# The residual of a channel MLP: turned to token layout by VectorE block transposes and SBUF moves in place of TensorE transposes

## The chip, the cores and the metric

The kernel runs on one core of one Trainium2 chip. The metric is the device time of one execution in microseconds (us). Unless marked ns, every time below is in us. All tensors that the engines compute with are 32-bit floats.

The engines are named as in the profile: PE is TensorE (PEld its weight loads), DVE is VectorE, ACT is ScalarE, POOL is GpSimd, SP is SyncE, which only issues transfers (DMAs). "SPq" and "ACTq" are the queues in which SP and ACT issue them.

## What is computed

```python
# 8 batch rows, 8 heads, 576 tokens, head size 64
scores = matmul(q, k.T) / 8
thresh = max(scores, -1) - tau
scores = where(scores >= thresh, scores, -1e9)
attn   = softmax(scores)                    # exp(scores - max) / (sum + 1e-9)
x      = matmul(attn, v)                    # heads side by side: (8, 576, 512)
# token MLP, over the 576 tokens of a row
u      = x + (relu(x.T @ w_tok1) @ w_tok2).T     # 576 -> 256 -> 576
# channel MLP, over the 512 channels of a token
out    = u + relu(u @ w_ch1) @ w_ch2             # 512 -> 1536 -> 512
```

What matters here is the last line: `u`, the residual, is needed twice. As input of the first channel product it is needed with the channels on the partitions; as addend of the output it is needed with the tokens on the partitions.

## The kernel before, in words

**Attention.** The work goes in 144 units (line 84): a batch row, a pair of head pairs, and one of 9 query tiles. Per unit, `scores` (L289) multiplies q and k for two heads into PSUM (L303), VectorE takes the row maxima (L308) and GpSimd makes the bias of them (L309). `weigh` (L312) has ScalarE apply the threshold (L318) and the exponential (L325); `norm` (L329) divides. The weights must then be turned. In row 0 TensorE does it (`turn`, L341). From row 1 on `turn_blocks` (L358) does it: VectorE transposes 32x32 blocks in place of their order (L366), and when three units are together 16 transfers on SP's queue (L375), one for each pair of block row and block column, carry the blocks to where they belong, from `T` to `eT`. `values` (L392) multiplies the turned weights with v (L410, L415) two units later; x comes out with channels on the partitions, in `xTs`, one tile for two batch rows.

**Token MLP.** `token_mlp` (L427) turns x on TensorE (L446), does the two products (L453, L463) and adds the result to x (L467). So `uT`, the residual, lies in `xTs` with channels on the partitions: 4 chunks of 128 channels, 1152 tokens of two rows.

**Channel MLP.** `channel_mlp` (L476) works on groups of 256 tokens (`GR`); two rows have 1152 tokens, so each pair of rows has four groups of 256 and one of 128. A group has 12 steps `ch1(j)` (L487, 128 of the 1536 hidden channels each, ReLU on ScalarE in L488) and, for each tile of 128 tokens, four steps `ch2(t, part)` with three of the 12 hidden chunks each (L503), which add up in one PSUM tile with the tokens on the partitions. Here is how the residual enters: in part 0, before the products, TensorE transposes the four 128x128 chunks of `uT` into this PSUM tile (L499, `start=(c == 0), stop=False`), and the products are added on top. After part 3, VectorE copies the tile to `o` (L508), and SP stores it (L509). There are 36 tiles of 128 tokens, thus 144 transposes. `o` has two buffers.

**Order.** The order of all instructions is written by hand. The MLP's steps stand in a queue `todo`, each with a cost (0.0067 us per token for a `ch1`, 2.6 or 3.0 us for a `ch2`). `fill` (L524) takes steps from it between the pieces of the attention's unit, to a quota per unit that `push` (L537) computes from the sum of the costs. So while the attention of row b runs, TensorE also does the MLPs of the rows before. What is left when the attention ends is done in one stretch (L655). Engines run their own instructions strictly in order, SP's queue too. q and k loads are issued by ScalarE from row 1 on (L644), v loads by SP (L646).

**Weights.** The MLP weights arrive as 64-bit floats and are converted in 31 pieces during rows 0 and 1, in steps on ScalarE (L192, L194), VectorE (L202, L204, L208) and GpSimd (L216). The raw words lie in a tile `scratch`, which has room for four pieces and 512 words more. One intermediate, `h2`, is written by L194 and read by L202 and L204; it is taken from the buffers of `o` (L180).

Of the kernel before, what the change touches and what calls it, by code (L numbers as in the profile page):

```python
# [9 lines left out]
F32 = mybir.dt.float32  # L10
# [7 lines left out]
P = 128  # L18
# [3 lines left out]
def kernel(  # L22
# [25 lines left out]
    nc = tc.nc  # L48
    B, H, S, D = q.shape
    DM = H * D  # L50
# [10 lines left out]
    NCC = DM // P  # L61
    NJ = DCH // P
    HS = S // 2
    NK = 2 * S // P
    GR = 2 * P
# [4 lines left out]
    work = ctx.enter_context(tc.tile_pool(name="work", bufs=2))  # L70
# [39 lines left out]
    def load_v(n):  # L110

        b, p = pairs[n]
        lv = ld.tile([P, NK, D], F32, tag="lv", bufs=4, name=f"lv_{n}")
        nc.sync.dma_start(out=lv, in_=v[b].rearrange("h s d -> (h s) d")[2 * S * p : 2 * S * p + 2 * S, :].rearrange("(c p) d -> p c d", p=P))
        vals[n] = lv
# [11 lines left out]
    wc2 = const.tile([P, NJ, DM], F32, name="wc2")  # L127
# [8 lines left out]
    WMAX = 512  # L136
    scratch = work.tile([P, NP * 2 * S], U32, tag="xT", name="scratch")
    NRAW = 4
    raw_at = [scratch[:, 2 * WMAX * i : 2 * WMAX * (i + 1)] for i in range(NRAW)]

    def like(x, dst):
        if len(dst.shape) == 2:
            return x
        return x.rearrange("p (a b) -> p a b", a=dst.shape[1])
# [23 lines left out]
    def load_piece(i):  # L168
        if i >= len(pieces):
            return  # L170
        dst, src = pieces[i]
        rows = dst.shape[0]
        n = 1
        for d in dst.shape[1:]:
            n *= d
        raw = raw_at[i % NRAW][0:rows, 0 : n * (2 if wide(i) else 1)].bitcast(src.dtype)
        nc.sync.dma_start(out=like(raw, dst), in_=src)
        if wide(i):
            words = raw.bitcast(U32).rearrange("p (n w) -> p n w", w=2)
            h2 = work.tile([P, WMAX], F32, tag="o", name=f"h2_{i}")[0:rows, 0:n]  # L180
            raws[i] = like(words[:, :, 0], dst), like(words[:, :, 1], dst), like(h2, dst)
        else:
            raws[i] = like(raw, dst)

    def wide(i):
        return i < len(pieces) and pieces[i][1].dtype == I64
# [37 lines left out]
    def weight(n):  # L224

        nonlocal steps_done
        for k in range(steps_done, min(steps_done + n, 3 * len(pieces) + 1)):
            i, part = divmod(k, 3)
            if part == 0:
                on_gpsimd(i - 1)  # L230
                if i:
                    load_piece(i - 1 + NRAW)
            else:
                on_scalar(i + 1, part - 1)
            on_vector(i, part)
            steps_done = k + 1

    def weight_to(x):

        weight(max(int(x) - steps_done, 0))  # L240

    def need(i):

        weight(3 * i + 4 - steps_done)

    load_piece(0)
    load_v(0)
    for i in range(1, NRAW):
        load_piece(i)
# [27 lines left out]
    def in_blocks(b):  # L277
        return b > 0
# [60 lines left out]
    GU = 3  # L339
# [87 lines left out]
    def token_mlp(b, ps=range(NP)):  # L427
# [45 lines left out]
        steps += [(0.97, lambda c=c, f=f: tok2(c, f)) for c in ps for f in range(2)]  # L473
        return steps, (first, first + NTK)

    def channel_mlp(b, uT, i):  # L476

        s = {}
        n = min(GR, 2 * S - GR * i)

        def ch1(j):
            need(7 + j)
            if j == 0:
                s["g"] = work.tile([P, NJ, GR], F32, tag="g", bufs=1, name=f"g_{b}_{i}")
            ps = ps_mm.tile([P, GR], F32, tag="mm", name=f"c1_{b}_{i}_{j}")[:, 0:n]
            for c in range(NCC):
                nc.tensor.matmul(ps, lhsT=wc1[:, j, c, :], rhs=uT[:, c, GR * i : GR * i + n], start=(c == 0), stop=(c == NCC - 1))  # L487
            nc.scalar.activation(out=s["g"][:, j, 0:n], in_=ps, func=AF.Relu)  # L488

        def ch2(t, part):  # L490
            need(7 + NJ + 3 * part + 2)
            t0 = GR * i + P * t
            if part == 0:
                s["ps"] = ps_mm.tile([P, NCC, P], F32, tag="mm", name=f"c2_{b}_{i}_{t}")
            ps = s["ps"]
            flat = ps.rearrange("q c d -> q (c d)")
            if part == 0:
                for c in range(NCC):
                    nc.tensor.matmul(  # L499
                        ps[:, c, :], lhsT=uT[:, c, t0 : t0 + P], rhs=ident, is_transpose=True, start=(c == 0), stop=False, skip_group_check=True  # L500
                    )
            for j in range(3 * part, 3 * part + 3):
                nc.tensor.matmul(  # L503
                    flat, lhsT=s["g"][:, j, P * t : P * t + P], rhs=wc2[:, j, :], start=False, stop=(j == NJ - 1), skip_group_check=True
                )
            if part == 3:
                o = work.tile([P, DM], F32, tag="o", name=f"o_{b}_{i}_{t}")
                nc.vector.tensor_copy(out=o, in_=flat)  # L508
                nc.sync.dma_start(out=out[b : b + 2].rearrange("b s d -> (b s) d")[t0 : t0 + P, :], in_=o)  # L509

        return [(0.0067 * n, lambda j=j: ch1(j)) for j in range(NJ)] + [
            (2.6 if part else 3.0, lambda t=t, part=part: ch2(t, part)) for t in range(n // P) for part in range(4)
        ]

# [43 lines left out]
    def values_due(u):  # L560
        while due and due[0][0] <= u:
            _, b, p0, g = due.popleft()
            values(b, p0, g)
            if b == 0 and p0 == 0 and g == 2:
                return True
            if p0 == NP - 2 and g == 2:
                if not in_blocks(b):
                    return True
                push(b)
        return False  # L570

    for u in range(len(units) + LAG + 4):
        on = u < len(units)
        if u == UB:
            late.close()
            ps_mm = ctx.enter_context(tc.tile_pool(name="ps_mm", bufs=2, space=bass.MemoryType.PSUM))
        if on:
            b_now, p0, t = units[u]
            n = b_now * NP + p0
        w = u - LAG  # L580
        back = 0 <= w < len(units)
        if on:
            scores(u)

        last = False
        visit = False
        if due and not in_blocks(due[0][1]):
            visit = due[0][0] <= u
            last = values_due(u)
        elif early:  # L590
            early.popleft()[1]()
        if 0 < u <= len(units):
            norm(u - 1)
        if b_now:
            weight(2)
        else:


            weight_to(2.25 * (u - (1 if visit else 1.5)))
            if visit and on:  # L600
                weigh(u)
        while copies:
            copies.popleft()()
        if last and u < UB:
            early.extend(token_mlp(0, range(NP // 2))[0])
        elif last:
            push(0)
        if back:
            wb, wp, wt = units[w]
            if not in_blocks(wb):  # L610
                for i in range(3):
                    turn(w, i)
            if wt % GU == GU - 1:
                g = wt // GU
                if g < 2:
                    split_middle(wb * NP + wp + g)
                due.append((u + (2 if in_blocks(wb) else 1), wb, wp, g))
        if b_now:
            fill(0.4)
        if back and in_blocks(wb):  # L620
            turn_blocks(w)
        if b_now:
            weight(2)
        if on and (b_now or not visit):
            weigh(u)
        elif b_now:
            fill(0.6)
        if b_now:
            weight(2)
        elif u == 0:  # L630
            on_scalar(0, 0)
            on_scalar(0, 1)
        else:
            weight_to(2.25 * (u - 1))
        if on:


            when = {3: (2, 0, 2), 4: (2, 2, 4), 5: (2, 4, 6), 6: (2, 6, 8), 8: (3, 0, 3), 0: (1, 3, 6), 1: (1, 6, 8)}
            if u == 0:
                load_qk(1, (nc.sync, nc.sync), range(0, 3))  # L640
            if t in when:
                m, lo, hi = when[t]
                if n + m < len(pairs):
                    load_qk(n + m, (nc.scalar if b_now else nc.sync,) * 2, range(lo, hi))  # L644
            if t in (3, 7) and n + 2 + t // 4 < len(pairs):
                load_v(n + 2 + t // 4)  # L646
            if t == 2:
                prep(n + 1)
            if t == 7 and n + 2 < len(pairs):
                prep(n + 2)  # L650
        if due and in_blocks(due[0][1]):
            values_due(u)
    need(len(pieces) - 1)
    quota = 1e9
    fill(1.0)  # L655
# [28 lines left out]
```

## Time and profile before

| | before |
|---|---|
| median of 3 runs (lowest to highest) | 1362.69 (1360.92 to 1366.38) |
| the profiled execution: its own time | 1362.23 |
| the profiled execution: span of the profile | 1360.1 |
| mean clock granted to TensorE | 0.996 |
| DVE, ACT, POOL busy, share of the span | 42%, 43%, 26% |
| the four heaviest lines of PE: L503, L487 (256 columns), L303 (128 columns), L415 (384 columns) | 390.6, 350.0, 172.5, 89.1 |
| the transposes of the residual, L499, x144: sum of their durations | 22.0 |
| copies to `o`, L508, x36: busy, mean | 24.7, 687 ns |
| attention's block transposes, L366, x126: busy, mean | 172.1, 1366 ns |

The span is the time from the first to the last record of one profiled execution; the execution's own time has some 2.1 us around it. A busy sum of TensorE counts the durations of overlapping instructions once per instruction in the groups, but the engine's total counts every instant once. A matmul's duration is not what it costs the engine, since the next one begins before it has ended; the distance from start to start is. In timelines a line gives the start in us, the length in us, then engine, line, operation and names; square brackets at the end give the idle time before it and who ended it. In views of waits a line reads: who waited, for whom, total us, number of times, longest.

### The profile page before, as it was taken

Reading aid. Unit: us, or ns where it says so; the run is one execution under the profiler, and the core shown is the slowest. Engines: PE = TensorE matmul, PEld = TensorE weight load, DVE = VectorE, ACT = ScalarE, POOL = GpSimd, SP = SyncE. Lnnn points to the kernel's source line nnn. Section 1 sums busy time; section 2 is a strip of 40 time slices with the busy share of each in tenths; the row PEclk is TensorE's granted clock in tenths of the full one; section 3 lists DMA queues with packets and bytes.
Section 4 is the critical chain, followed back from the end, with each engine's and each line's share of the span. In section 5 each row is a group of like instructions: output and inputs, shape, how many; then the busy total and the mean of one; then the engine's idle time right before and its main releaser. Section 6 shows DMA issues by size and latency. Waiting matters only on the chain.

```text
span 1360.1 us, 17717 instructions
## 1 busy us (share of the span) xinstructions
PE 1315.2 (97%) x6246; PEld 817.2 (60%) x6246; DVE 575.3 (42%) x1009; ACT 584.3 (43%) x1299; POOL 353.6 (26%) x683
## 2 busy tenths in 40 slices
PE   6888899999999999999999999999999999999998
PEld 4555556547474666655665566565756566576675
DVE  5878874445443434443333454434333443201000
ACT  6776664445454444543434445353434444120010
POOL 4666653222222222221212222222212222100000
PEclk9999999999999999999999999999999999999999
DMA  5434774545453533533244444435333442400000
GB/s 122 109 92 129 196 170 102 127 95 127 96 130 77 134 89 84 135 76 92 66 112 99 104 97 114 95 76 118 90 90 74 114 99 70 111 0 16 8 16 16
DMA packets 278871, 128.20 MB, mean 94 GB/s; under 512 B 200896, under 2 KB 271552, under 8 KB 278784
## 3 DMA queue, kind: packets, MB, share of 16 engines
q1 hardware_dynamic: 150176, 111.06, 32.0%
q10 hardware_dynamic: 128608, 16.01, 7.4%
q8 instruction: 50, 0.82, 0.3%
q14 instruction: 37, 0.30, 0.1%
HBM read 43.25 MB, written 9.44 MB: 39 GB/s over the span
## 4 chain that ended last, share of the span: by engine, by line
PE 89%; DVE 4%; DMA 2%; ACT 2%; issue 1%; SPq 1%; POOL 1%; ACTq 0%; DVEq 0%; POOLq 0%
PE c L503 28%; PE c L487 27%; PE sc L303 11%; PE pv L415 8%; PE t L453 5%; PE t L463 4%; PE pv L410 3%; DVE mx L308 2%; PE c L499 1%; PE tx L446 1%; PE tr L354 1%; ACT e L318 1%; SPq L375 1%; DMA eT<-T 1%; DMA lk<-in_k_dram 1%
## 5 line engine op out<-in xcount | busy, mean ns | idle before, releaser
L308 DVE TENSOR_REDUCE mx<-sc 128x1 f32<-128x576 f32 x288 | 204.5, 750 | 484.6 <-PE sc L303 484.6
L487 PE MATMUL c<-xT,wc 128*128 128x256 f32 (+1 forms) x1920 | 400.3, 362 | 0.1
L503 PE MATMUL c<-wc,g 128*128 128x512 f32 x864 | 390.6, 597 | 0.0
L487 PEld LDWEIGHTS c<-xT,wc 128*128 128x128 f32 x1920 | 334.4, 191 | 70.5 <-issue 31.5
L309 POOL TENSOR_SCALAR bias<-mx,toff 128x1 f32<-128x1 f32 x288 | 81.9, 284 | 781.2 <-DVE mx L308 724.3
L318 ACT ACTIVATE e<-sc,bias 128x576 f32<-128x576 f32 x288 | 199.4, 740 | 157.5 <-POOL bias L309 153.5
L503 PEld LDWEIGHTS c<-wc,g 128*128 128x128 f32 x864 | 157.4, 190 | 175.4 <-issue 173.7
L488 ACT ACTIVATE g<-c 128x256 f32<-128x256 f32 (+1 forms) x240 | 86.8, 362 | 321.4 <-PE c L487 308.6
L325 ACT ACTIVATE e<-e,ntau 128x576 f32<-128x576 f32 x288 | 221.1, 772 | 0.0
L336 POOL TENSOR_SCALAR e<-e,rr 128x576 f32<-128x576 f32 x288 | 214.6, 757 | 14.7 <-DVE rr L333 2.8
L303 PE MATMUL sc<-kT,qT 64*128 64x288 f32 (+1 forms) x1280 | 193.5, 441 | 11.9 <-DVE kT L285 7.2
L366 DVE STREAM_TRANSPOSE T<-e 128x1152 f32<-128x1152 f32 x126 | 172.1, 1366 | 5.8 <-DMA eT<-T 3.6
L303 PEld LDWEIGHTS sc<-kT,qT 64*128 64x128 f32 (+1 forms) x1280 | 106.2, 181 | 99.2 <-issue 61.8
L415 PE MATMUL pv<-eT,lv 128*64 128x384 f32 (+1 forms) x1024 | 136.2, 406 | 0.0
L415 PEld LDWEIGHTS pv<-eT,lv 128*64 128x64 f32 x1024 | 75.2, 137 | 49.3 <-issue 40.4
L508 DVE COPY o<-c 128x512 f32<-128x512 f32 x36 | 24.7, 687 | 169.7 <-PE c L503 169.7
L420 ACT COPY xT<-pv 128x384 f32<-128x384 f32 (+1 forms) x56 | 21.0, 400 | 166.2 <-PE pv L415 165.2
L463 PE MATMUL t<-w,a 128*128 128x288 f32 x256 | 73.6, 414 | 5.7 <-DVE xT L467 4.8
L453 PE MATMUL t<-x_sb,w 128*128 128x512 f32 (+1 forms) x180 | 73.4, 555 | 0.0
L467 DVE TENSOR_TENSOR xT<-xT,t 128x288 f32<-128x288 f32 x64 | 28.4, 448 | 86.6 <-PE t L463 86.0
L463 PEld LDWEIGHTS t<-w,a 128*128 128x128 f32 x256 | 45.5, 190 | 28.0 <-issue 11.7
L325 ACT ACTIVATION_READ_ACCUMULATOR e<-e,ntau 128x1 f32 x288 | 56.8, 197 | 0.0
(44 smaller groups left out, 547.2 us busy)
## 6 DMA issues: line engine op xcount, KB each, us to landing
eT<-T SPq DMA_DIRECT2D x672, 108.0 KB, 2.3
scratch<-in_moe_w_ch_dram SPq DMA_DIRECT2D x24, 512.0 KB, 3.8
lv<-in_v_dram SPq DMA_DIRECT2D x32, 288.0 KB, 3.5
out_dram<-o SPq DMA_DIRECT2D x36, 256.0 KB, 2.2
lk<-in_k_dram ACTq DMA_DIRECT2D x111, 72.0 KB, 2.7
lq<-in_q_dram ACTq DMA_DIRECT2D x106, 72.0 KB, 2.3
lq<-in_q_dram SPq DMA_DIRECT2D x22, 72.0 KB, 3.2
lk<-in_k_dram SPq DMA_DIRECT2D x17, 72.0 KB, 3.4
```

What stands on the lines that cost most here:

```text
L303: nc.tensor.matmul(sc[h][rows, f, 0:HS], lhsT=qT[r, cols], rhs=kT[r, HS * f : HS * f + HS], start=True, stop=True)
L308: nc.vector.tensor_reduce(out=mx[:, c], in_=sc[h][:, :, 0:HS], axis=AX.XY, op=ALU.max)
L318: nc.scalar.activation(out=eh, in_=sc[h][:, :, 0:HS], func=AF.Prelu, bias=bias[:, h : h + 1], scale=SCALE, alpha=STEEP)
L325: nc.scalar.activation(out=eh, in_=eh, func=AF.Exp, bias=ntau, accum_out=rs[:, h : h + 1])
L336: nc.gpsimd.tensor_scalar(out=eh, in0=eh, scalar1=rr[:, h : h + 1], scalar2=1.0, op0=ALU.mult, op1=ALU.mult)
L366: nc.vector.transpose(out=T[:, :, place, :].rearrange("p a (c x) -> p c a x", c=NK), in_=e.rearrange("p (c a x) -> p c a x", c=NK, a=4))
L415: nc.tensor.matmul(to[r], lhsT=lv[:, j, :], rhs=e[j], start=False, stop=(c == NI - 1), skip_group_check=True)
L453: nc.tensor.matmul(to, lhsT=w1[:, t, P * m : P * m + P], rhs=x_sb[:, t, cols], start=(t == 0), stop=(t == NT - 1))
L463: nc.tensor.matmul(to, lhsT=a[:, m, P * c : P * c + P], rhs=w2[:, m, HS * f : HS * f + HS], start=(m == 0), stop=(m == NTK - 1))
L487: nc.tensor.matmul(ps, lhsT=wc1[:, j, c, :], rhs=uT[:, c, GR * i : GR * i + n], start=(c == 0), stop=(c == NCC - 1))
L488: nc.scalar.activation(out=s["g"][:, j, 0:n], in_=ps, func=AF.Relu)
L503: nc.tensor.matmul(flat, lhsT=s["g"][:, j, P * t : P * t + P], rhs=wc2[:, j, :], start=False, stop=(j == NJ - 1), skip_group_check=True)
```

## The change

From the third batch row on (`b` is 2, 4 or 6 in `channel_mlp`, which counts pairs of rows), the four transposes on TensorE are left out, and the first product begins the PSUM tile. In their place, `turn_u` transposes the 32x32 blocks of the group's `uT` on VectorE into a tile `us`, at the step `ch1(1)`. It puts 16 moves in a list; each carries a block row and a block column from `us` to `ut`. The list is emptied to SP's queue by `move_u`: at the end of the first of each three attention units, at the end of every unit once no new scores are begun, and before the first eviction that needs them. At the eviction VectorE adds PSUM and `ut` in one instruction and writes to `us`, whose own content has been moved by then; the store reads it there. `us` and `ut` have one buffer each, for a whole group of up to two tiles. Rows 0 and 1 keep the transposes and the copy, but their copy goes to `us` as well.

The buffers of `o` are gone. `h2` therefore moves to the 512 spare words of `scratch`, of which there is one in place of two.

```diff
+    high = scratch[:, 2 * WMAX * NRAW : 2 * WMAX * NRAW + WMAX].bitcast(F32)
...
-            h2 = work.tile([P, WMAX], F32, tag="o", name=f"h2_{i}")[0:rows, 0:n]
+            h2 = high[0:rows, 0:n]
...
+    moves = deque()
+
     def channel_mlp(b, uT, i):
 
         s = {}
         n = min(GR, 2 * S - GR * i)
+        nt = n // P
+
+        def turn_u():
+
+            us, ut = s["us"], s["ut"]
+            nc.vector.transpose(
+                out=us[:, 0:nt].rearrange("q n a (c d) -> q c (n a) d", c=NCC),
+                in_=uT[:, :, GR * i : GR * i + n].rearrange("q c (m r) -> q c m r", r=32),
+            )
+
+            def move(a, k):
+                nc.sync.dma_start(out=ut[32 * a : 32 * a + 32, 0:nt, k, :], in_=us[32 * k : 32 * k + 32, 0:nt, a, :])
+
+            moves.extend([lambda a=a, k=k: move(a, k) for a in range(4) for k in range(4)])
...
             nc.scalar.activation(out=s["g"][:, j, 0:n], in_=ps, func=AF.Relu)
+            if j == 1:
+                s["us"] = work.tile([P, GR // P, 4, NCC * 32], F32, tag="us", bufs=1, name=f"us_{b}_{i}")
+                if b:
+                    s["ut"] = work.tile([P, GR // P, 4, NCC * 32], F32, tag="ut", bufs=1, name=f"ut_{b}_{i}")
+                    turn_u()
...
-            if part == 0:
+            if part == 0 and not b:
                 for c in range(NCC):
                     nc.tensor.matmul(
                         ps[:, c, :], lhsT=uT[:, c, t0 : t0 + P], rhs=ident, is_transpose=True, start=(c == 0), stop=False, skip_group_check=True
                     )
...
-                    flat, lhsT=s["g"][:, j, P * t : P * t + P], rhs=wc2[:, j, :], start=False, stop=(j == NJ - 1), skip_group_check=True
+                    start=(j == 0 and b > 0),
...
-                o = work.tile([P, DM], F32, tag="o", name=f"o_{b}_{i}_{t}")
-                nc.vector.tensor_copy(out=o, in_=flat)
+                o = s["us"][:, t].rearrange("q a x -> q (a x)")
+                if b:
+                    move_u()
+                    nc.vector.tensor_add(
+                        out=o.rearrange("q (c k d) -> q c k d", c=NCC, k=4),
+                        in0=ps.rearrange("q c (k d) -> q c k d", k=4),
+                        in1=s["ut"][:, t].rearrange("q k (c d) -> q c k d", c=NCC),
+                    )
+                else:
+                    nc.vector.tensor_copy(out=o, in_=flat)
                 nc.sync.dma_start(out=out[b : b + 2].rearrange("b s d -> (b s) d")[t0 : t0 + P, :], in_=o)
 
-            (2.6 if part else 3.0, lambda t=t, part=part: ch2(t, part)) for t in range(n // P) for part in range(4)
+            (2.6 if part or b else 3.0, lambda t=t, part=part: ch2(t, part)) for t in range(nt) for part in range(4)
         ]
+
+    def move_u():
+        while moves:
+            moves.popleft()()
...
         if due and in_blocks(due[0][1]):
             values_due(u)
+
+        if back and wt % GU == 0 or not on:
+            move_u()
```

More of the change, by code (lines that the diff above doesn't have):

```diff
@@ L503, in ch2 @@
                 nc.tensor.matmul(
-                    flat, lhsT=s["g"][:, j, P * t : P * t + P], rhs=wc2[:, j, :], start=False, stop=(j == NJ - 1), skip_group_check=True
+                    flat,
+                    lhsT=s["g"][:, j, P * t : P * t + P],
+                    rhs=wc2[:, j, :],
+                    start=(j == 0 and b > 0),
+                    stop=(j == NJ - 1),
+                    skip_group_check=True,
                 )
             if part == 3:
-                o = work.tile([P, DM], F32, tag="o", name=f"o_{b}_{i}_{t}")
-                nc.vector.tensor_copy(out=o, in_=flat)
+                o = s["us"][:, t].rearrange("q a x -> q (a x)")
[8 more added lines that the diff above has]
+                    nc.vector.tensor_copy(out=o, in_=flat)
                 nc.sync.dma_start(out=out[b : b + 2].rearrange("b s d -> (b s) d")[t0 : t0 + P, :], in_=o)
         return [(0.0067 * n, lambda j=j: ch1(j)) for j in range(NJ)] + [
-            (2.6 if part else 3.0, lambda t=t, part=part: ch2(t, part)) for t in range(n // P) for part in range(4)
+            (2.6 if part or b else 3.0, lambda t=t, part=part: ch2(t, part)) for t in range(nt) for part in range(4)
         ]
+    def move_u():
+        while moves:
+            moves.popleft()()
     KEEP = 45.0
```

## Prediction

> **What bounds the kernel now.** I read the busy times first, then the stretches, then TensorE's waits, and last the places the edit touches.
>
> ```profile
> PE 1315.2 (97%) x6246; PEld 817.2 (60%) x6246; DVE 575.3 (42%) x1009; ACT 584.3 (43%) x1299; POOL 353.6 (26%) x683
> ```
>
> By stretches (length, busy us and instructions of PE, PEld, DVE, ACT, POOL, clock, DMA share, GB/s):
>
> ```profile
> 0.00:170.00 170.00, 137.24 (x740) 88.78 (x740) 133.42 (x262) 117.64 (x246) 98.36 (x152) 0.97 0.52 130
> 170.00:1190.00 1020.00, 1011.92 (x4857) 618.59 (x4858) 433.45 (x733) 445.75 (x1001) 255.25 (x531) 1.00 0.44 102
> 1190.00:1360.10 170.10, 166.05 (x652) 109.84 (x648) 8.47 (x15) 20.94 (x54) 0.00 (x0) 1.00 0.03 11
> ```
>
> TensorE is idle 45 us: 33 in batch 0, 4 at the end, and 8 in the 1020 us that hold nearly all of the edit. There a microsecond less of TensorE work is a microsecond less of time, unless a new wait takes it back. What TensorE waits for there (total us, times, longest):
>
> ```profile
> PE pv L410 <- DMA lq<-in_q_dram: 1.9, 1, 1.9
> ...
> PE pv L410 <- DMA eT<-T: 0.2, 1, 0.2
> ```
>
> The value products (L410, L415) hardly wait for the attention's own moves (L375). How close that is decides below. The moves' issues and landing, and the outputs' issues (ns min/median/max):
>
> ```profile
> L375 SPq DMA_DIRECT2D eT<-T x672: 585/602/2106, 142.0 to 1186.5; - x168
> ...
> DMA to landing us min/median/max: 2.2/2.3/4.5
> ```
>
> ```profile
> L509 SPq DMA_DIRECT2D out_dram<-o x36: 332/362/1652, 201.6 to 1356.8; - x36
> ```
>
> SP's queue in time (start, us): a set of 16 takes 10.3 to 13.2 us, not 16 x 0.60 = 9.6, as some issues wait for a completion semaphore:
>
> ```profile
> 708.36 10.67 SPq L375 DMA_DIRECT2D eT<-T  x16
> 719.14 0.54 SPq L114 DMA_DIRECT2D lv<-in_v_dram  x1
> 736.97 12.04 SPq L375 DMA_DIRECT2D eT<-T  x16
> 749.12 0.53 SPq L509 DMA_DIRECT2D out_dram<-o  x1
> ```
>
> **What the skill says.** (1) "TensorE: Matmul & The Clock Gate", Part 4: a TensorE transpose lasts about 275 ns in a kernel, most of it access latency. The trace agrees on the duration (273 ns median for L499), but durations overlap, so it isn't the cost. (2) "VectorE: DVE Perf Modes", The three transpose paths: VectorE transposes only within 32x32 blocks. Hence 16 moves finish a 128x128 turn, as the attention's L366 and L375 show. (3) "DMA: Bandwidth & Descriptors", Anatomy of one DMA: about 2 us are fixed in a transfer, and a wait is served by the issuing sequencer before dispatch. The trace agrees: 2.3 us to landing, and a late item holds SP. (4) "Perfetto Trace Analysis", DMA Instruction — HWDGE: the profiled window of an issue holds lock wait, generation and push, not the data movement. So 0.60 us is what a move takes of SP.
>
> **Part 1: 108 transposes leave TensorE.** Rows 0 and 1 have 9 token tiles, rows 2 to 7 have 27, each with four L499. The price is read where TensorE runs without a gap (start, duration):
>
> ```profile
> 1281.34 0.60 PE L499 MATMUL c<-ident,xT 128*128 128x128 f32 x4
> 1281.77 10.46 PE L503 MATMUL c<-wc,g 128*128 128x512 f32 x24
> ```
>
> From start to start four take 0.43 us. 27 x 0.43 = **11.6 us less**. The sum of durations (22.0 us, 27/36 of it 16.5) counts the overlap twice; both ends for the range are 11 and 13. The fill costs fall with it (3.0 to 2.6), so the pace stays matched.
>
> **Part 2: VectorE.** The eviction copy becomes an add with one PSUM input. The copy of 512 is 0.69 us; the add L467 of 288 is 0.45, of which a copy's slope (384 in 0.55, 192 in 0.34: 1.1 ns per element) makes 0.69 at 512. Taken: 0; bounds 0 to 0.3 us each, and only the last of 27 is on the path. New block transposes: L366 does 1152 in 1.36 us and L285 576 in 0.75, so 1024 take 1.23 us: 12 of 1.23 and 3 of 0.7 are 17 us of VectorE. It is busy 433 of 1020 us and idle 4.5 us on average before each pair of maxima (330.2 us in 73 waits from 500 to 1190), so this is hidden; uncovered it would cost up to 17.
>
> **Part 3: the transpose waits for the outputs.** us and ut have one buffer. In the changed instruction order VectorE's turn of the next group stands behind the last add of the previous one, and must wait until the output read of us has landed. Of the 15 turns, 11 come while attention runs. Four of these find the output landed. Four have only one T transpose between: 0.36 + 2.2 - 1.36 = 1.2 us of wait. Three have the output queued behind a set of eT moves: about 12 + 0.4 + 2.2 us after T, against one unit of 8.4 us (125 T transposes in 1051.5 us), so 4 to 6 us. Behind them on VectorE stand the next maxima, and behind those POOL's bias, ScalarE's Prelu and TensorE's next scores but one. The cover is VectorE's 4.5 us, and TensorE's own slack: e.g. maxima at 676.75, Prelu done at 679.31, next scores at 685.01, 5.7 us. Taken: 0. Bounds: 0 to 11 x 1 us. The four late turns stand in a stretch without attention; the last group's moves have 27 us of ch1 and ch2 before the add in a full group, and in the short last one its 16 x 0.6 + 2.3 = 12 us fit in the 21 us that 1334.4 to 1355.6 leave.
>
> **Part 4: 240 moves on SP.** The move isn't in the trace: lower bound an output's 0.36 us, nearest row L375's 0.60, with waits 0.75 (12/16); upper 2.1, L375's maximum. Taken 0.65: 10.4 us per group. They stand behind the eT set that ends before, and semaphores are handed round between SP's and ScalarE's DMAs in program order, so a move also waits for the loads issued ahead (from 480 to 1190 us SP waits 24.9 us in 14 cases for an lq load). SP's period of three units is 3 x 8.4 = 25.2 us: eT set 11.5, moves 10.4, two outputs and lv 1.3, is 23.2, so 2 us remain. Behind the moves are the next eT set, out and lv, and ScalarE's q/k loads that reuse a semaphore. What a late eT set costs: from 480 to 1190 I could place 24 sets; from set end plus 2.3 us to the L410 that reads it is 3.5 us on average, but under 1.9 in seven. A late set is thus not free everywhere. Periods run from 21 to 32 us, so some of the 11 groups overflow by 1 to 4 us and some of that meets a short margin. Taken: 11 x 0.25 = **3 us more**; bounds 0 and (rival 1, 2) 10 and above.
>
> **Part 5: one h2 instead of two.** The weight conversion on ScalarE (L194) now waits until VectorE has read h2 for the piece before (L204). Pairing the 31 of each, 13 of 30 starts lie before that point, by 0.07 to 2.7 us, 14 us in all. The largest, ScalarE then VectorE:
>
> ```profile
> 47.16 0.47 ACT L194 ACTIVATE h<-scratch 128x288 f32<-128x288 f32 x1
> 49.10 1.56 ACT L318 ACTIVATE e<-sc,bias 128x576 f32<-128x576 f32 x2 [1.47 <-POOL bias L309]
> ```
>
> ```profile
> 49.56 0.29 DVE L204 TENSOR_SCALAR w<-h 128x288 uint32<-128x288 uint32 x1
> ```
>
> L194 moves from 47.16 to 49.85, L318 from 49.10 to 50.3. Most others run into a ScalarE wait that was there (2.95 us at 119.18, 2.14 at 137.90, 6.95 at 157.17). Taken: **0.5 us more**; bounds 0 and 14, the second if all batch 0 followed.
>
> **Sum.** -11.6 + 0 + 0 + 3 + 0.5 = -8.1. The profiled execution took 1362.2 us (span 1360.1, 2.1 around it), so 1354.1. The median of the runs is 1362.7, 0.5 higher; minus 8.1 it is 1354.6. I say 1354.4.
>
> **Rivals.** *Likeliest, 0.53:* the covers hold as above; 1351 (nothing given back) to 1356. *Rival 1, 0.31, the saving becomes a DMA wait:* each of 11 groups delays an eT set by about 1 us over its margin, through SP's queue or a ScalarE load waiting for a move's semaphore. For it: 2 us of room, seven margins under 1.9. Against: only 11 of about 36 periods carry moves, the next ones catch up. Price: 11 x 0.9 = 10 in place of 3, 1354.4 + 7 = 1361; 1356 to 1367. *Rival 2, 0.16, slower, SP overruns:* one mechanism, moves that cost over 1.1 us each. At 1.15 a group takes 18.4; 11.5 + 18.4 + 1.3 = 31.2 is 6.0 over the period, less 3.5 of margin is 2.5 x 11 = 28 us; 1362.7 - 11.6 + 0.5 + 28 = 1380. It decides from 1.1 us per move (30.4, 5.2 late, 1.7 x 11 = 19). For it: maximum 2.1 us. Against: the median of 0.60 at a larger size (108 KB against 32).
>
> **How the numbers follow.** Under 0.5%, 6.8 us, a measurement here tells nothing. Faster (below 1355.9) is the likeliest case with its upper end cut and a little of rival 1: 0.54. Same is the rest of rival 1 and some of both neighbours: 0.32. Slower, rival 2 less its start: 0.14. The range reaches from 13 us of saving with nothing given back, 1350, to most of rival 1, 1364; it leaves about 0.18, rival 2 nearly all of it.
>
> **What would show it.** L499 x36 instead of 144; PE busy in 170 to 1190 still over 99% of the stretch; a move at 0.5 to 0.75 us of SP; L410 waiting for eT under 4 us in all; the turn waiting for out in seven places; TensorE idle in batch 0 grown by under 1 us. Wrong if L410 or the scores wait 8 us or more, if ScalarE stands on its loads, or if the first stretch grows.

## The result, and the profile after

| | before | after |
|---|---|---|
| median of 6 runs (lowest to highest) | 1361.99 (1360.92 to 1366.38) | 1355.22 (1353.73 to 1358.86) |
| ratio, with its 95% interval | | 0.9948 (0.993 to 0.9967) |
| the profiled execution: its own time, its span | 1362.23, 1360.1 | 1356.31, 1354.5 |

The change gains 6.8 us, half a per cent. Up to L308 a line of the kernel after has the number of before plus one; further down the residual's old transposes (L499) are L524, the two channel products (L487, L503) are L507 and L528, the copy of rows 0 and 1 is L546 and the store L547. New are the turn on VectorE (L491), the moves (L497) and the add (L540). The busy times of the whole program after the change:

```profile
PE 1308.3 (97%) x6138; PEld 810.6 (60%) x6138; DVE 591.7 (44%) x1024; ACT 585.5 (43%) x1299; POOL 355.2 (26%) x683
```

TensorE lost 108 instructions and 6.9 us of busy time, VectorE took 16.4 us more, and the others are as they were. The stretches of after, in the columns of the prediction's table (length, busy us and instructions of PE, PEld, DVE, ACT, POOL, clock, DMA share, GB/s):

```profile
0.00:170.00 170.00, 138.56 (x745) 89.72 (x746) 134.16 (x261) 119.08 (x248) 98.29 (x152) 0.96 0.52 130
170.00:1190.00 1020.00, 1009.05 (x4789) 614.71 (x4787) 445.86 (x746) 446.10 (x999) 256.95 (x532) 1.00 0.46 107
1190.00:1354.50 164.50, 160.72 (x608) 106.12 (x607) 11.68 (x18) 20.31 (x53) 0.00 (x0) 1.00 0.07 23
```

In the middle stretch TensorE's idle time went from 8.1 to 10.95 us: its work got shorter, and a few us of new waiting came in. TensorE's waits of this stretch that matter below (who waited, for whom, total us, times, longest), after and then before:

```profile
PE t L464 <- ACT g L508: 3.2, 3, 1.6
PE pv L411 <- DMA lk<-in_k_dram: 2.6, 1, 2.6
...
PE pv L411 <- DMA eT<-T: 0.4, 1, 0.4
```

```profile
PE t L463 <- ACT g L488: 0.8, 1, 0.8
```

The value products waited 0.4 us for the attention's moves, where 0.2 had been: the feared wait is not there. But L464 (L463 before), the second product of the token MLP, waited three times for a ReLU on ScalarE, 3.2 us in all; before, it was one time, 0.8. The prediction had not looked at that line. The moves' own view (issues in ns min/median/max; then the time to landing) and SP's queue at the place that the prediction showed:

```profile
L497 SPq DMA_DIRECT2D ut<-us x240: 507/594/1625, 511.1 to 1343.4; - x120
...
DMA to landing us min/median/max: 1.7/1.9/3.7
```

```profile
714.88 3.83 SPq L376 DMA_DIRECT2D eT<-T  x6
718.76 15.19 SPq L497 DMA_DIRECT2D ut<-us  x16
734.04 0.54 SPq L114 DMA_DIRECT2D lv<-in_v_dram  x1
735.45 10.29 SPq L376 DMA_DIRECT2D eT<-T  x16
```

A move takes 0.59 us of SP, and the 16 moves of a group lie back to back with the next set of eT (733.95 to 735.45, with one v load between). So SP is indeed full here, but the set still lands in time: the last of it landed 5.1 us before the first value product that reads it.

**Where the time came from and where it went.** The 36 evictions (L508 before; L546 and L540 after) are the same milestones in every kernel, in the order of VectorE. The table gives, for the profiled executions, the start of an eviction in a kernel less its start in before, with the difference at the eighth eviction (before: 441.04 us; the eighth of the nine tiles of rows 0 and 1) set to zero. The 27 tiles that have the new path are evictions 10 to 36.

| eviction, counted from 1 (start in before) | 9 (495.44) | 17 (759.57) | 18 (812.67) | 25 (1057.28) | 26 (1072.41) | 27 (1130.10) | 29 (1184.74) | 36 (1356.09) |
|---|---|---|---|---|---|---|---|---|
| after | +1.56 | -2.25 | -0.95 | -4.28 | +0.49 | -3.33 | -4.21 | -8.22 |
| after, taken again | +1.56 | -2.39 | -1.08 | -3.84 | +0.92 | -3.06 | -3.93 | -7.95 |
| 108 transposes left out, nothing in place | +1.56 | -2.94 | -1.63 | -4.96 | -0.26 | -4.18 | -5.05 | -9.07 |
| the declared costs alone | +1.55 | +0.38 | +2.13 | +1.72 | +6.74 | +3.76 | +3.76 | +2.77 |
| after, with the old costs | -0.01 | -3.43 | -3.86 | -7.20 | -7.63 | -8.07 | -8.94 | -12.29 |

From 29 to 36, where next to no attention is left, the seven tiles gain 4.0 us in after and 3.4 with the old costs. The difference lies in the middle: after loses 1.56 us ahead of the first new tile (the declared costs alone, without the new path, lose the same 1.56) and 1.3 between 17 and 18, and the two tiles from 25 to 27 together lose 0.95 where the old costs gain 0.87. The last row, which keeps one number of the source as before, has none of that. The experiments show why.

### The profile page after: what moved, and what is told of

It is laid out like the page before. It is cut to its first block, busy times and chain, and to the rows that moved or that the text cites. A ratio compares the mean times of both kernels' runs of the same rounds, so it can differ in the third digit from the quotient of the medians.

```text
span 1354.5 us, 17794 instructions
## 1 busy us (share of the span) xinstructions
PE 1308.3 (97%) x6138; PEld 810.6 (60%) x6138; DVE 591.7 (44%) x1024; ACT 585.5 (43%) x1299; POOL 355.2 (26%) x683
## 4 chain that ended last, share of the span: by engine, by line
PE 87%; DVE 5%; ACT 3%; DMA 2%; SPq 1%; issue 1%; POOL 1%; ACTq 0%; DVEq 0%; POOLq 0%
PE c L507 27%; PE c L528 27%; PE sc L304 11%; PE pv L416 9%; PE t L454 5%; PE t L464 4%; PE pv L411 3%; DVE mx L309 2%; ACT e L319 1%; PE tx L447 1%; SPq L376 1%; PE tr L355 1%; DMA lk<-in_k_dram 1%; ACT e L326 1%; DVE wc L205 0%
## 5 line engine op out<-in xcount | busy, mean ns | idle before, releaser
L507 PE MATMUL c<-xT,wc 128*128 128x256 f32 (+1 forms) x1920 | 400.0, 362 | 0.1
L528 PE MATMUL c<-wc,g 128*128 128x512 f32 x864 | 389.5, 597 | 0.0
L507 PEld LDWEIGHTS c<-xT,wc 128*128 128x128 f32 x1920 | 334.3, 190 | 69.8 <-issue 29.7
L319 ACT ACTIVATE e<-sc,bias 128x576 f32<-128x576 f32 x288 | 199.5, 740 | 178.7 <-POOL bias L310 178.0
L528 PEld LDWEIGHTS c<-wc,g 128*128 128x128 f32 x864 | 158.9, 190 | 181.6 <-issue 178.1
L508 ACT ACTIVATE g<-c 128x256 f32<-128x256 f32 (+1 forms) x240 | 87.0, 362 | 295.9 <-PE c L507 285.8
L540 DVE TENSOR_TENSOR us<-c,ut 128x512 f32<-128x512 f32 x27 | 18.6, 690 | 155.0 <-PE c L528 140.3
L464 PE MATMUL t<-w,a 128*128 128x288 f32 x256 | 75.2, 421 | 8.0 <-DVE xT L468 4.7
L464 PEld LDWEIGHTS t<-w,a 128*128 128x128 f32 x256 | 45.8, 192 | 30.1 <-issue 10.5
```

What stands on the lines that cost most here:

```text
L319: nc.scalar.activation(out=eh, in_=sc[h][:, :, 0:HS], func=AF.Prelu, bias=bias[:, h : h + 1], scale=SCALE, alpha=STEEP)
L464: nc.tensor.matmul(to, lhsT=a[:, m, P * c : P * c + P], rhs=w2[:, m, HS * f : HS * f + HS], start=(m == 0), stop=(m == NTK - 1))
L528: nc.tensor.matmul(flat, lhsT=s["g"][:, j, P * t : P * t + P], rhs=wc2[:, j, :], start=(j == 0 and b > 0), stop=(j == NJ - 1), skip_group_ ...
```

## The experiments

Two theories stood against each other for what keeps the gain below 27 x 0.43 = 11.6 us: the new work (moves on SP, the turn's waits, the shared h2), as the prediction's Parts 3 to 5 have it; or the order of TensorE's steps, which the lowered cost of a `ch2` changes. A third was chance in the start-up. The expectations, quoted as they were written before each run, set these against each other.

**The change again.** No edit.

> The changed kernel once more, unchanged, to see what of its profile recurs. Theory A (rows 0 and 1 are hurt by the one h2 buffer, and by a long wait of L411 near 248 us after which TensorE's clock drops): 0.993 to 0.997 of before, the eviction near 441 us comes 2 to 3 us later than before, the products behind the wait near 250 us are slow again. Theory B (the loss in rows 0 and 1 is chance of one execution): that eviction within 1 us of before, or the slow products absent, and a ratio of 0.992 or less.

Measured: 1354.26 against 1363.12, ratio 0.9941 (0.9927 to 0.9955). From the eighth eviction on its profile follows the first one to within half a microsecond (second row of the table), so what happens there belongs to the kernel. What lies ahead of it doesn't: the eighth eviction came 2.89 us late in the first profile of after and 0.46 us late in this one. Times of rows 0 and 1 are therefore not used to judge an edit of a later row.

**The transposes left out, nothing in their place.** The residual is missing from rows 2 to 7; the costs are lowered as in the change.

```diff
-            if part == 0:
+            if part == 0 and not b:
...
-start=False
+start=(j == 0 and b > 0)
...
-            (2.6 if part else 3.0,
+            (2.6 if part or b else 3.0,
```

> The kernel before with the 108 transposes of rows 2 to 7 left out and nothing in their place (the residual is missing from the output of these rows). It measures the saving alone. Theory A (0.43 us per token tile, nothing hidden): 11.6 us less, ratio 0.9915, 0.990 to 0.993. Theory B (part of the transposes was hidden in gaps, and this, not a new wait, is why the change brought 7): 6 to 8 us less, ratio 0.9945 to 0.9955.

Measured: 1354.5, ratio 0.994 (0.9927 to 0.9953), the same as the change. There is no move, no turn and no add of `ut` in this kernel, and yet it gains no more in its median, and loses at the same places (third row of the table). From eviction 8 to 36 it gains 9.07 us where after gains 8.22 and, taken again, 7.95. So in this stretch all the new work together costs about 1 us, and more than 2 us of the missing gain has another cause.

**One h2 alone**, in before, and **two h2** in the change.

```diff
+    high = scratch[:, 2 * WMAX * NRAW : 2 * WMAX * NRAW + WMAX].bitcast(F32)
...
-            h2 = work.tile([P, WMAX], F32, tag="o", name=f"h2_{i}")[0:rows, 0:n]
+            h2 = high[0:rows, 0:n]
```

```diff
-    high = scratch[:, 2 * WMAX * NRAW : 2 * WMAX * NRAW + WMAX].bitcast(F32)
+    pair = work.tile([P, 2, WMAX], F32, tag="ut", bufs=1, name="h2")
...
-            h2 = high[0:rows, 0:n]
+            h2 = pair[0:rows, i % 2, 0:n]
```

> The kernel before with the one h2 buffer alone. Theory A (it makes ScalarE wait, and rows 0 and 1 come 1 to 3 us later): ratio 1.001 to 1.002; ScalarE waits for L205-like reads of h2 for about 11 us in all. Theory B (these waits are all hidden, the loss in rows 0 and 1 is something else): ratio 0.9995 to 1.0005 with the same waits on ScalarE.

> The changed kernel with two h2 buffers again (they lie in the buffer of ut, which is unused until row 2). Theory A: 1 to 3 us faster than the changed kernel, ratio to before 0.992 to 0.994. Theory B: no difference from the changed kernel, 0.9945 to 0.996.

Measured: 1363.44, ratio 1.0002 (0.9994 to 1.0011) for the first, 1354.74, ratio 0.9943 (0.9931 to 0.9955) for the second. The shared h2 costs nothing that can be measured, neither alone nor in the change. Its waits are there all the same. ScalarE's waits in after:

```profile
ACT scratch L195 <- DVE wc L205: 7.3, 8, 1.9
...
ACT scratch L195 <- DVE w L205: 3.6, 2, 2.6
```

**The old costs, in the change.** One number: the first part of a `ch2` is declared at 3.0 again for all rows.

```diff
-            (2.6 if part or b else 3.0,
+            (2.6 if part else 3.0,
```

> The changed kernel with the old declared cost of the first ch2 step, 3.0 for every row, so that TensorE's order is that of before with 27 groups of four transposes gone and nothing else moved. Theory C (the 3.4 us that are missing were lost because the lower cost, 2.6, moved the steps of the token MLP against the attention's units, so that TensorE waits in new places): 11 to 12 us less than before, ratio 0.991 to 0.992, and 2.5 to 3.5 us below the changed kernel; the stretches between evictions 7-8, 16-17 and 25-26 have the idle time of before. Theory D (new DMA or ScalarE waits from the edit itself took them): 0.994 as the changed kernel.

Measured: 1350.74, ratio 0.9924 (0.9903 to 0.9945). The gain from eviction 8 to 36 is 12.29 us, half as much again as in after. TensorE's instructions now stand in the order of before, less the 27 groups of transposes: with the residual's transposes taken out of both, the 6102 remaining products of the two profiles follow each other in the same order.

**The costs alone**, in before: transposes and copies stay, only the declared costs are lowered.

```diff
-            (2.6 if part else 3.0,
+            (2.6 if part or b else 3.0,
```

> The kernel before with nothing but the declared cost of the first ch2 step lowered to 2.6 from row 2 on; all 144 transposes stay. TensorE's order is then that of the changed kernel plus the transposes. Theory C: 2 to 4 us slower than before, ratio 1.0015 to 1.003, with new idle time of TensorE (L463 waiting for L488) in the stretches where the changed kernel had it. Theory D (the lower cost matters only because the work got shorter): no difference, 0.9995 to 1.0005.

Measured: 1365.16 against 1363.32, ratio 1.0016 (1.0005 to 1.0027), so about 2 us slower (1.8 by the medians, 2.2 by the ratio), and 2.77 in the stretch. It is small, but the interval excludes no change, and the profile has the same marks at the same places as after. The view of L463 (L464 in the later numbering), in the lines on what its engine waited for ahead of it (us, times; weight loads counted with the products), sorts the kernels into two kinds. First the declared costs alone, then after with the old costs:

```profile
  ACT g L488: 7.4, 7
```

```profile
  ACT g L508: 2.2, 3
```

Before has 2.2 in 3 as well; after, after again and the kernel with the transposes left out have 7.4 in 7. What happens is seen around eviction 17. After the change, TensorE, and below it ScalarE in the same microseconds:

```profile
772.11 2.05 PE L507 MATMUL c<-xT,wc 128*128 128x128 f32 x16
774.99 1.24 PE L464 MATMUL t<-w,a 128*128 128x288 f32 x4 [0.83 <-ACT g L508]
```

```profile
773.37 1.41 ACT L319 ACTIVATE e<-sc,bias 128x576 f32<-128x576 f32 x2 [0.97 <-POOL bias L310]
774.67 0.27 ACT L508 ACTIVATE g<-c 128x128 f32<-128x128 f32 x1
```

With the old costs, ScalarE at the same step:

```profile
771.69 0.28 ACT L508 ACTIVATE g<-c 128x128 f32<-128x128 f32 x1 [0.15 <-PE c L507]
771.86 1.36 ACT L319 ACTIVATE e<-sc,bias 128x576 f32<-128x576 f32 x2
```

`fill` hands out the MLP's steps to a quota in declared costs. With other costs the same steps fall at other places between the attention's pieces. Here a ReLU that ran ahead of the next unit's pair of Prelus (L319) now stands behind it in ScalarE's queue, and TensorE, which by the profile waits for this ReLU (done at 774.94) before its next product (774.99), stands still for 0.83 us. The other two such waits of after, 1.58 us ahead of 459.47 and 0.83 us ahead of 1091.63, look the same: the ReLU stands behind a pair of Prelus (at 459 us behind an exponential too). The price isn't only in the idle time. From eviction 17 to 18, in the groups of TensorE's lines, the 32 products of that line in after and with the old costs:

```profile
L464 PE MATMUL t<-w,a 128*128 128x288 f32 x32 | 9.7, 426 | 1.0 <-ACT g L508 0.8
```

```profile
L464 PE MATMUL t<-w,a 128*128 128x288 f32 x32 | 9.1, 406 | 0.0
```

That stretch takes 54.40 us against 52.67 with the same 290 products: 1.04 us of idle time and 0.69 of longer busy time, 0.6 of it in these 32: six of them, each the first of four, took 510 ns in place of 406, and with the old costs none did. So part of the loss shows as longer instructions, not as idle time.

**Left out, with the old costs.** The kernel with the transposes left out (rows 2 to 7 without the residual), costs as in before.

```diff
-            if part == 0:
+            if part == 0 and not b:
...
-start=False
+start=(j == 0 and b > 0)
```

> The transposes of rows 2 to 7 left out with nothing in their place (their residual is missing from the output), with the old declared costs. It gives the full saving without any wait of the replacement. Theory C: 11.6 us less, ratio 0.9915, within 0.001; what the changed kernel with old costs lies above it is the price of moves and VectorE work, by theory C 0 to 1 us. Theory D: the saving itself is only 8 us, ratio 0.994.

Measured: 1351.08, ratio 0.9916 (0.9899 to 0.9933); 12.30 us in the stretch. With the old costs in both, doing the residual the new way (12.29) and not doing it at all (12.30) take the same time: in these profiles the new work is hidden to the last tenth (two executions of after with the old costs, 12.29 and 12.05, differ by more). Nor was a part of the saving hidden in gaps, the second theory on the left-out kernel. And 12.30 over 27 tiles is 0.456 each; per tile the difference is 0.43 or 0.44 at nearly every eviction, with 0.3 us more at two places (20 to 21 and 29 to 30), where TensorE was idle for 0.23 and 0.92 us before and is for 0 and 0.60 now.

**Twice as many moves.** Each move is cut in two by channels: 384 of 16 KB and, in the three groups of 128 tokens, 96 of 8 KB, in place of 192 of 32 and 48 of 16.

```diff
-                nc.sync.dma_start(out=ut[32 * a : 32 * a + 32, 0:nt, k, :], in_=us[32 * k : 32 * k + 32, 0:nt, a, :])
+                for c in (0, 64):
+                    nc.sync.dma_start(out=ut[32 * a : 32 * a + 32, 0:nt, k, c : c + 64], in_=us[32 * k : 32 * k + 32, 0:nt, a, c : c + 64])
```

> The changed kernel with every move cut in two by channels (480 moves of 16 KB in place of 240 of 32 KB, the same bytes). It doubles the time of SP's queue for a group to some 20 to 24 us. By the prediction's rival of an overrun (period 25.2 us, eT set 11.5, other issues 1.3, mean margin 3.5): 8 to 12 us late, less 3.5, in 11 groups, 45 to 90 us slower than the changed kernel, ratio 1.03 to 1.06. Theory A (the backlog meets periods without moves and the measured margins, and only part of it is seen): 5 to 30 us slower, 0.998 to 1.016. A third, that SP's queue is no limit at all: under 2 us.

Measured: 1428.08, ratio 1.0482 (1.0465 to 1.05), 73 us over after. The moves' issues, and what waits now (TensorE, then VectorE):

```profile
L498 SPq DMA_DIRECT2D ut<-us x480: 507/594/1672, 509.0 to 1419.6; - x160
```

```profile
PE pv L411 <- DMA eT<-T: 39.9, 8, 9.5
```

```profile
DVE us L541 <- DMA ut<-us: 59.2, 5, 22.5
```

Half the bytes cost SP the same 594 ns, so a group's set takes about twice the time (20.9 us at 509.0; the 15 sets take 20.4 to 26.5, where in after they take 10.2 to 15.9). That overruns the period, and the wait lands where Rival 2 put it, on the value products. Its formula, with 20.9 to 23.4 us for a set (two that were read), gives 11.5 + 20.9 + 1.3 - 25.2 - 3.5 = 5.0, and with 23.4 7.5 us, in each of 11 groups, 55 to 83 us. The 39.9 us that L411 waits are not all of it: SP's lateness also holds VectorE's adds, and the mean clock of TensorE fell from 0.994 to 0.977.

**The turn later.** At `ch1(4)` in place of `ch1(1)`, so that the stores have landed.

```diff
-            if j == 1:
+            if j == 4:
```

> The changed kernel with the turn at ch1(4) in place of ch1(1), when the stored output has landed; the wait of VectorE (28 us in 7 waits) should fall below 8 us. Theory A (this wait is covered and costs nothing): the time of the changed kernel within 1 us, 0.9935 to 0.9955. Rival (it delays scores): 2 to 5 us faster. The moves come later too; if the adds then wait for them, up to 3 us slower.

Measured: 1354.61, ratio 0.9941 (0.9929 to 0.9954), as after. VectorE's waits for the stores, in after and in this kernel:

```profile
DVE us L491 <- DMA out_dram<-us: 28.4, 7, 8.3
```

```profile
DVE us L491 <- DMA out_dram<-us: 13.5, 6, 2.6
```

Half the wait is gone, and the median moved by less than the spread of the runs. In the stretch this kernel gains 8.76 us, where after gained 8.22 and 7.95: if the wait cost anything, it was half a microsecond, about what two executions of one kernel differ by.

**The new path for all rows, with the old costs.**

```diff
-            if part == 0 and not b:
+            if False:
...
-            (2.6 if part or b else 3.0,
+            (2.6 if part else 3.0,
```

(`if b:` ahead of the turn and of the add becomes `if True:`, and every first product begins its tile, `start=(j == 0)`)

> The new path for all rows, 0 and 1 too, with the old declared costs: 36 more transposes gone, 80 more moves. By 0.44 us per tile another 4.0 us: 1346.5 to 1348, ratio 0.9885, if SP's queue and VectorE have room in rows 2 and 3 as they had later; if the moves meet the margins of the eT sets there, no gain or up to 5 us worse than the old costs alone.

Measured: 1370.56, ratio 1.0058 (1.0042 to 1.0073). Nine more tiles at 0.43 would have been a gain of 3.9 us; instead it lost 19 us to the version without them, and the expectation missed. The eighth eviction is 22.45 us late; from there it gains as the others (12.15 us to the last). From 170 to 450 us TensorE is idle 21.3 us, where before it was 5.95, and its granted clock there is 0.96, where before had 1.00. Its longest waits in these 280 us:

```profile
PE c L507 <- ACT g L508: 9.4, 2, 7.9
PE pv L411 <- DMA eT<-T: 4.4, 2, 3.8
PE pv L411 <- DMA lv<-in_v_dram: 4.2, 1, 4.2
```

So here the value products do wait for the attention's moves, as the expectation's second case has it, but 4.4 us are the smaller part. There SP still carries the weights' loads and ScalarE their conversion; in the whole run the turn waits 52.2 us for stores in ten places, and ScalarE 22.1 us in eight for k loads. Which of these is the first cause wasn't told apart.

**The best version again.** The change with the old costs, as above.

> The changed kernel with the old declared costs once more, beside the two above on one chip: ratio 0.991 to 0.9925, 3 to 4 us below what the changed kernel showed.

Measured: 1351.6, ratio 0.992 (0.9905 to 0.9935). Both executions agree, 1350.74 and 1351.6. This is the fastest kernel found, about 12 us below before and some 3 to 4 below the change as made. The intervals of these ratios overlap, so that last figure rests on the milestones (12.29 and 12.05 against 8.22 and 7.95 us) more than on any one pair of medians. The runs together say the same: the five measurements with the lowered cost and some of the transposes gone have ratios of 0.9940 to 0.9948 (after twice, left out, two h2, the later turn), the three with the old cost 0.9916 to 0.9924.

## Why the prediction was right in its sum and wrong in its terms

The predicted 1354.4 and the measured 1355.22 lie close, and the mechanism of the gain held. But two terms were wrong and cancelled: nothing was allowed for the pace, which cost about 3 us, and 3.5 us for waits that cost about 1 or nothing.

**What the saving is worth (Part 1, -11.6): right.** Read from start to start, 0.43 us per tile; measured 0.43 to 0.44 per tile, 12.3 us for 27 with the order kept. The sum of the durations (16.5) would have been too high by a third.

**"The fill costs fall with it (3.0 to 2.6), so the pace stays matched": this is the step that failed.** The lowered costs keep the sum of the costs true to the work, but they also move steps. The runs give about 2 us (costs alone, ratio 1.0016), 2.8 us (the same in the stretch), 3.2 us (the two kernels with the transposes left out, 9.07 against 12.30) and 4.1 us (after less the version with old costs, where the price of the new work is in it too). In all three places where the token MLP's second product (L464) holds up TensorE for a ReLU, the ReLU stands behind a pair of Prelus on ScalarE. Of the 4.1 us, idle time of TensorE makes 2.75 (4.36 us from eviction 8 to 36 in after, 1.61 with the old costs: 8 to 9, 1.58 against 0.97; 9 to 10, 0.21 against 0; 17 to 18, 1.04 against 0; 25 to 26, 0.43 against 0; 26 to 27, 1.06 against 0; and 0 against 0.60 between 29 and 30); the rest is in longer instructions, resolved for one stretch only. One of the prediction's own signs told of it: TensorE was to be busy over 99% of the stretch from 170 to 1190 us, and was 98.9% (99.2% before and with the old costs). The declared cost read as a description of the work; it is also an instruction to the order.

**VectorE (Part 2, 0): right.** The turn takes 1.245 us (1.23 estimated), the add 0.69 (0.69), and the engine has 16.4 us more to do (17).

**The turn's wait (Part 3, 0): right in cost, low in size.** The prediction saw three waits of 4 to 6 us and four of 1.2 while the attention runs; the trace has three there of 8.0, 8.3 and 3.3 us and three of 0.8 to 1.0, the latter put down to VectorE's own transposes. The four late turns wait 2.1 to 2.3 us each, for which the prediction gave no figure. In the first wait one sees what stands behind the turn: the scores were done at 504.47 us, and their maxima began at 510.99, after the turn (509.82). VectorE's adds wait as well, 14.8 us in three places, the longest 10.5, by the profile for eT transfers, which lie on SP's queue with the moves; the prediction had looked at that only for the tail. The later turn shows that the cover holds, to within half a microsecond.

**SP's moves (Part 4, 3): mis-sized.** The issue alone was right (0.65 taken, 0.594 median), but some wait, so that a set takes 10.2 to 15.9 us, 12.5 on average, where 10.4 was taken; the attention's own sets before took up to 14.9 us, not 13.2. By the prediction's own sum (11.5 + 12.5 + 1.3 against 25.2) the room is gone, and L411's wait for eT grew from 0.2 to 0.4 us. Yet with the old costs the work costs 0.0 (12.29 against 12.30), with the lowered ones about 1 (8.22 and 7.95 against 9.07). What each move set does to the set of eT behind it can be followed where the order is that of before: in the 11 places the last eT transfer landed 1.5 to 6.4 us before the first product that reads it, and with the moves and the old costs 1.1 to 6.2, 0.1 less on average and at most 2.3 less in one place. So the margins of the sets behind the moves are used in part and nowhere used up; with the lowered costs the smallest is 0.2 us. The 3 us put a price on an overflow that the margins took in.

**One h2 (Part 5, 0.5): nothing that can be measured.** 10.9 us of waits in ten places, where 14 in 13 were counted. None of it shows at the end, but the interval of the run with h2 alone reaches 1.0011, 1.5 us, so the half microsecond is not excluded.

**The rivals.** Rival 1 fell: no eT wait of any size in the change. Rival 2 did not come about, since a move costs 0.59 us, 0.78 with the waits in its set, and its threshold is 1.1; the doubled moves, at 1.3 to 1.7 us for each pair, cross it and land where it said. Neither rival, nor any step, had the order of the steps as a cause.

## What to carry to other kernels

Where steps are interleaved to declared costs, a cost is a knob of the order: after removing work, time both the lowered and the old cost, since the old order may be the better tuned one. Judge a small change by milestones that every kernel has, from a point behind the part that varies, and take the work away without putting anything in its place to see what its replacement costs. A sum that comes out right does not show that its terms are right.

## What was not expected of the hardware

**An issue is priced by the piece.** The median issue takes 594 ns of SP for the moves of 32 and of 16 KB as they are and 594 for the halves; the attention's of 108 KB take 602, and the stores of 256 KB 362. So it isn't the size that sets it. Cutting moves to make them smaller cost 73 us. The Trainium skill, "DMA: Bandwidth & Descriptors", Anatomy of one DMA, which the prediction draws on, fits its 2 us to transfers that GpSimd issues; for SP's the trace decides, 1.9 us to landing for these moves and 2.3 for the attention's.

**A wait can cost twice.** The start-up varied between executions at one spot near 248 us, where the value products wait for a set of eT. The profile names loads of q and k as what ended the wait, but these products read eT, and the last eT transfer landed at 248.51 us before and at 249.67 after, 0.14 and 0.13 us ahead of them. Before, then after:

```profile
248.65 0.55 PE L410 MATMUL pv<-eT,vl 128*64 128x192 f32 x4 [1.92 <-DMA lq<-in_q_dram]
249.00 1.50 PE L415 MATMUL pv<-eT,lv 128*64 128x192 f32 x16
```

```profile
249.80 0.91 PE L411 MATMUL pv<-eT,vl 128*64 128x192 f32 x4 [2.58 <-DMA lk<-in_k_dram]
250.47 2.64 PE L416 MATMUL pv<-eT,lv 128*64 128x192 f32 x16
```

The wait is 0.66 us longer, and the same 16 products then take 2.64 us in place of 1.50; the granted clock from 241 to 251 us is 0.92 where before had 1.00. The Trainium skill, "TensorE: Matmul & The Clock Gate", Why this matters for your kernels, says to keep gaps of TensorE under about 3 us, since the clock falls after one. These traces agree that the clock falls after gaps, but the length of a gap doesn't settle it. The second execution of the change had a gap of 2.39 us at this spot and kept the clock at 1.00; the kernel with h2 alone had 2.44, and its 16 products took 2.83 us. A gap of 3.05 us ahead of 139.54 left the clock of before at 1.00 for the next 4 us, while one of 2.90 ahead of 140.67 in after was followed by a mean of 0.63. What decides between them was not found. The fall isn't caused by the change (of its two executions one had it), and it is one reason why the eighth eviction differs between them: of the 2.43 us, 0.95 were there when these products began, and 1.14 are the slower products.

**What stays open.** Most of the pacing loss that lies in busy time was resolved only between evictions 17 and 18. A version with two buffers of `us` was not tried. What sets the new path back in rows 0 and 1 was not told apart. All profiles are single executions; only the change and the version with old costs were profiled twice.
